# A sparse mixture's row scatters in four groups of four behind VectorE's work of four slots, and its gate's steps up to seven slots sooner

## The chip, the cores and the metric

One core of a Trainium2 chip runs the whole program in one launch. The metric is the time of one execution on the device in microseconds, taken as the median of several runs; lower is better. One further execution was recorded by the hardware profiler, and every row below is of that one.

## The reference, cut to what matters

Eight batches of attention between 512 positions and 32 states, in both directions, give 544 rows a batch, 4352 in all, of 512 numbers. A dense gated layer follows, and then a sparse one that sends every row to the one of eight experts with the largest logit.

```python
x = np.ascontiguousarray(attn_out.transpose(0, 2, 1, 3)).reshape(B * S, H * D)
a = x @ w_a
b = x @ w_b
x = (a * b @ w_out).astype(np.float32)
logits = x @ w_gate
e_idx = np.argmax(logits, axis=1)
gate_w = probs[np.arange(N), e_idx]
eom = 1.0 / (1.0 + np.exp(-(x @ w_output_gate)))
for e in range(E):
    mask = e_idx == e
    h = np.maximum(x[mask] @ w1[e], 0.0)
    ye = h @ w2[e]
    out[mask] = gate_w[mask, None] * eom[mask, e, None] * ye
```

Here probs is the softmax of the logits. All is float32; the kernel splits each factor of a large product into a high and a low part and adds three matmuls.

## The kernel before, in words

Phase 1 (class Phase1) does attention, the dense layer and the gate of the sparse layer; Phase 2 does the experts. Between them rows go through `ysort`, a table in memory that is sorted by expert: phase 1 scatters each row to its place there, phase 2 fetches the rows of one expert as blocks.

**A batch.** `main(b)` works through twelve blocks f of 128 hidden columns. `s1(b, f)` makes the two hidden products of the block on TensorE into `ps_ab` (12 matmuls each, L627); ScalarE copies one (`a`, L589), VectorE multiplies it by the other (L593), ScalarE rounds the result to the high part `gh` (L597), VectorE makes the low part `gl` (L601). `s2` (L646) adds the block's part of the output into the four banks `ps_y`. Each pair of blocks needs `Mh` and `Ml`, which `mprep` makes from the state and the weights: matmuls into two auxiliary banks `ps_m` (L566), ScalarE's copy `Mh` (L326), VectorE's difference `Ml` (L327).

**Slots.** Between these stand 24 slots, one behind each s1 and one behind each s2. `main` fills a list `prog` of 24 lists with small units of other work, and `slots` runs the units of the next slot each time that it is called. By the tables of `CFG`, `at` gives the slots of the next batch's attention (turning x, scores `ps_s`, softmax, the transposes `ps_e` at L486, the read of the states `ps_sr`), `gate` those of the gate of the batch before; the `ps_m` of the next pairs come every four slots, that of the next batch in slot 20. The scheduler keeps this order nearly as written on each engine, and moves an instruction only where its inputs are there sooner or later. All the small matmuls and transposes take turns in the two auxiliary banks of `ps_x`.

**The gate.** `gate(b, T)` returns nine units for T tiles of 128 rows: two that turn the output back into rows (`blocks`, in tile `y`, L810); `logits` (`ps_l`, L818); `gather` (transposes `ps_lt`, L831, and the sum L836); `pick` (the largest logit as a 0/1 row `oh`, L846 to L861); `osel` (the other gate's logit; GpSimd's running counts per expert, `cum` and `gpre`, L875 and L876); `scale` (the row's factor, L883 to L887, and the row's number, copied by GpSimd, L888); `pos` (place in the table: matmuls `ps_pos`, L895 and L898, and VectorE's L903 to L913); and `spread`. This last makes the places and factors stand where the rows stand (matmul `ps_sp`, L920), gets the places `gdu` as whole numbers (L924), writes the factors into the rows (L927), and has GpSimd issue 4T scatters of 128 pieces of 130 numbers each (L292):

```python
    def scatter(self, **kw):

        self.disjoint(self.nc.gpsimd.indirect_dma_start(**kw))
...
            nc.vector.tensor_copy(out=blocks[:, :, RB - 2 : RB - 1], in_=ps[:, n : 2 * n].unsqueeze(2))
            for t in range(n):
                self.scatter(
```

So a gate of four tiles issues sixteen scatters one behind the other, and L888 of the next gate, on the same queue, waits for all of them. The turns L810 of the next gate write the tile that they read, and wait for them too.

**Behind the batches.** `main_sr` runs the dense layer for the 256 rows that the states read, with the gate of the last batch in its own slots (`side`). Then comes a stage written out by hand in `moe_kernel`, with the gate of those 256 rows (two tiles, eight scatters in one unit, run inside `pre1(2)`), the table of the steps, and the first expert blocks; last `Phase2.run` loops over the other blocks.

`mark`, `follow`: `mark` gives the place in the program written so far, `follow(i, last)` keeps instruction i behind `last` on its engine without a wait.

Of the kernel before, what the change touches and what calls it, by code (L numbers as in the profile page):

```python
# [19 lines left out]
NB = 8  # L20
# [13 lines left out]
RB = DM // 4 + 2  # L34
# [10 lines left out]
    "conv": [0, 0, 0, 0, 0, 0, 0, 0, 0, 0, 1, 1, 1, 0, 1, 1, 1, 0, 0, 1, 0, 0, 0, 0],  # L45
    "at0": [12, 14, 13, 13, 15, 16, 16, 18, 18, 20, 21, 23, 23, 23],
    "at": [6, 7, 9, 10, 11, 13, 14, 17, 18, 15, 19, 21, 22, 23],
    "gate": [1, 2, 2, 5, 6, 7, 9, 10, 14],
    "u0": [10, 10, 11, 11],
    "sr0": 1,  # L50
    "mp0": 3,
# [4 lines left out]
class Phase1:  # L56
# [662 lines left out]
    def main_sr(self):  # L719
        nc, p1, p2 = self.nc, self.p1, self.p2  # L720
        n = self.nb * NS
        sh = p1.tile([P, 4, n], F32R, name="srh")
        sl_ = p1.tile([P, 4, n], F32R, name="srl")
        for j in range(4):
            self.split(sh[:, j, :], sl_[:, j, :], self.srT[:, j, :])
        g = self.gate(self.nb - 1, 4)
        choose, w1 = self.moe2.early()
        side = [[]] * CFG["sr0"] + [g[0:3], g[3:4], g[4:6], g[6:8], g[8:9], [choose]]
        side += [[]] * (18 - len(side)) + [[lambda j=j: w1(j)] for j in range(4)]
        aux = self.slots(side, 2 * NFC)  # L730
        gts = {}
        ys = [self.ps_y.tile([P, 512], F32, tag=f"y{t}", name=f"ps_y{t}")[:, 0:n] for t in range(4)]

        def wsplit(f):
            r = []
            for ab in range(2):
                h, l = (self.p3.tile([P, 4, P], F32R, tag=t, name=t) for t in ("wh", "wl"))
                self.split(h, l, self.wab[:, ab, :, P * f : P * f + P])
                r.append((h, l))
            return r  # L740

        w = wsplit(0)
        for f in range(NFC + 1):
            if f == NFC - 3:
                at = self.mark()
            if f < NFC:
                pab = []
                for ab in range(2):
                    ps = self.ps_ab.tile([P, 512], F32, tag="ab", name=f"ps_sab{ab}")
                    i = 0  # L750
                    wh, wl = w[ab]
                    for m, r in ((wh, sh), (wh, sl_), (wl, sh)):
                        for j in range(4):
                            nc.tensor.matmul(  # L754
                                out=ps[:, 0:n], lhsT=m[:, j, :], rhs=r[:, j, 0:n], start=i == 0, stop=i == 11
                            )
                            i += 1
                    pab.append(ps)
                if f + 1 < NFC:
                    w = wsplit(f + 1)  # L760
                gts[f] = self.product(pab[0], pab[1], n, f)
                next(aux)
            if f:
                self.s2(ys, gts.pop(f - 1), f - 1)
                next(aux, None)
        for _ in aux:
            pass
        for c, y in enumerate(ys):
            nc.scalar.activation(out=self.yTf[:, F2 + n * c : F2 + n * c + n], in_=y, func=AF.Copy)
        self.pin(at, nc.scalar, nc.vector)  # L770
# [29 lines left out]
    def gate(self, b, T):  # L800
        nc, p1, p2 = self.nc, self.p1, self.p2
        ident = self.ident
        st = {}

        yT = self.yT if T == 4 else self.yTf[:, 4 * T * P :].rearrange("p (c n) -> p c n", c=4)
        blocks = self.y[:, 0 : 4 * T]

        def turn(*cs):
            for c in cs:
                nc.vector.transpose(  # L810
                    out=blocks[:, :, 32 * c : 32 * c + 32], in_=yT[:, c, :].rearrange("p (t i) -> p t i", i=32)
                )
# [104 lines left out]
        def spread():  # L917
            n = 4 * T
            ps = self.aux("ps_sp")
            nc.tensor.matmul(  # L920
                out=ps[:, 0 : 2 * n], lhsT=self.turnto, rhs=st["z"].rearrange("p t g -> p (t g)"), start=True, stop=True
            )
            du = sm("gdu", [n], U32)
            nc.vector.tensor_scalar(  # L924
                out=du, in0=ps[:, 0:n], scalar1=4.0, scalar2=self.aoff[:, 0:1], op0=ALU.mult, op1=ALU.add
            )
            nc.vector.tensor_copy(out=blocks[:, :, RB - 2 : RB - 1], in_=ps[:, n : 2 * n].unsqueeze(2))  # L927
            for t in range(n):
                self.scatter(
                    out=self.ysort.rearrange("r (a w) -> (r a) w", a=4),  # L930
                    out_offset=bass.IndirectOffsetOnAxis(ap=du[:, t : t + 1], axis=0),
                    in_=blocks[:, t, :],
                    in_offset=None,
                    bounds_check=4 * NE * CAP - 1,
                    oob_is_err=False,
                )

        return [lambda: turn(0, 1), lambda: turn(2, 3), logits, gather, pick, osel, scale, pos, spread]


ds = bass.ds
# [11 lines left out]
class Phase2:  # L953
# [131 lines left out]
    def turn(self, e, y):  # L1085
        return e.transpose(out=self.yts, in_=y)
# [847 lines left out]
def moe_kernel(tc, x, state, w_a, w_b, w_out, w_gate, w_og, w1, w2, out):  # L1934
    w_a, w_b, w_out = (w.bitcast(I32) for w in (w_a, w_b, w_out))
    with ExitStack() as ctx:
# [5 lines left out]
        ph.run(ctx, m)  # L1942
        m.tiles(ctx)
        at = ph.mark()
        turn0, turn1, logits, gather, pick, osel, scale, pos, spread = ph.gate(NB, 2)
        table = m.table(cp)
        w2 = lambda c: m.wsplit(0, m.raw1[:, 1], c)
        turn = lambda i: m.turn(tc.nc.vector, m.yin[i])
# [15 lines left out]
        scale()  # L1964
        pos()
        stage()
        m.pre1(2, {6: spread})
        stage()
        m.fetch_pre(2)
        m.pre2(-2, 1)  # L1970
# [60 lines left out]
```

## Time and profile before

| what | us |
| --- | --- |
| median of 3 runs | 1182.87 |
| lowest and highest of them | 1180.47, 1192.52 |
| the profiled execution | 1190.98 |
| its span, from the first to the last instruction | 1189.3 |

TensorE's mean granted clock in the profiled execution was 0.978. A row of a timeline gives the start in us, the duration in us, the engine, the line, the operation with output and inputs, how many instructions were joined, and in brackets the idle time of the engine ahead of it with what ended that. Tiles go by their names in the program. A releaser "issue" means that the engine waited for nothing that the profile shows, "remote" that no event on this core was found for it. Matmuls overlap, so TensorE's durations add up to more than the time between starts.

### The profile page before, as it was taken

How to read it: one execution, taken by the hardware profiler on the slowest of the kernel's cores; microseconds unless marked ns; L12 is line 12 of the kernel's file. 1: busy time of each engine (PE TensorE's matmuls, PEld its weight loads, DVE VectorE, ACT ScalarE, POOL GpSimd, SP SyncE). 2: the span in 40 equal slices, each digit the busy share in tenths (PEclk: the TensorE clock that was granted, in tenths of full speed). 3: DMA queues.
4: the chain of work that ended last, by engine and by line, in shares of the span. 5: the costliest groups of instructions: out<-in, count | busy, mean ns of one | idle time of the engine just before them, and what ended most of it. 6: DMA issues, size and time to landing. Idle time of an engine off the chain costs nothing.

```text
span 1189.3 us, 19341 instructions
## 1 busy us (share of the span) xinstructions
PE 1127.1 (95%) x7032; PEld 900.1 (76%) x7032; DVE 627.6 (53%) x1108; ACT 431.8 (36%) x703; POOL 287.7 (24%) x393
## 2 busy tenths in 40 slices
PE   5999999999999989999999897989999999999996
PEld 3766776776777766767767686878899998989884
DVE  5987464465645634743654262773353354445455
ACT  6875333333333423333342232521231233233233
POOL 6000032050060240230410532122133212233111
PEclk7999999999999999999999997999999999999998
DMA  8653202103013022010000126237363143737421
GB/s 306 232 180 67 43 17 74 21 30 78 3 47 64 7 65 37 14 59 1 28 10 1 37 43 171 90 116 176 115 144 114 53 108 105 179 82 191 95 97 31
DMA packets 99519, 99.11 MB, mean 83 GB/s; under 512 B 60096, under 2 KB 71392, under 8 KB 99360
## 3 DMA queue, kind: packets, MB, share of 16 engines
q1 hardware_dynamic: 87976, 71.56, 22.3%
q0 software_dynamic: 11120, 25.52, 7.5%
q8 instruction: 82, 1.34, 0.5%
q14 instruction: 77, 0.63, 0.2%
q10 hardware_dynamic: 264, 0.07, 0.0%
HBM read 76.75 MB, written 21.02 MB: 82 GB/s over the span
## 4 chain that ended last, share of the span: by engine, by line
PE 84%; another core or an unknown queue 4%; DVE 4%; ACT 3%; issue 2%; DMA 2%; POOLq 0%; SPq 0%; DVEq 0%; POOL 0%; ACTq 0%
PE ps_ab L627 21%; PE ps_y L646 21%; PE ps_h L1149 15%; PE ps_o L1170 14%; PE ps_m L566 4%; PE ps_sab L754 2%; PE ps_h L1622 1%; PE ps_o L1622 1%; PE ps_l L818 1%; DMA yT<-in_moe_w_b 1%; PE ps_sr L501 1%; PE ps_e L486 1%; DMA y<-in_moe_w_a 1%; PE ps_s L368 1%
## 5 line engine op out<-in xcount | busy, mean ns | idle before, releaser
L1149 PE MATMUL ps_h<-yT,w 128*128 128x256 f32 x1536 | 196.7, 285 | 9.3 <-issue 5.1
L1149 PEld LDWEIGHTS ps_h<-yT,w 128*128 128x128 f32 x1536 | 192.7, 192 | 16.1 <-issue 6.0
L1170 PE MATMUL ps_o<-w,hT 128*128 (+1 forms) x768 | 188.5, 394 | 0.0
L292 POOL DMA_INDIRECT ysort<-y,gdu x136 | 149.1, 1097 | 149.0 <-DVE y L927 105.4
L646 PE MATMUL ps_y<-gh,wo_h 128*128 128x512 f32 (+1 forms) x432 | 167.8, 392 | 1.3 <-issue 0.7
L646 PE MATMUL ps_y<-gh,wo_l 128*128 128x512 f32 (+1 forms) x432 | 164.3, 384 | 0.6 <-issue 0.5
L646 PE MATMUL ps_y<-gl,wo_h 128*128 128x512 f32 (+1 forms) x432 | 163.0, 382 | 0.3 <-issue 0.3
L1170 PEld LDWEIGHTS ps_o<-w,hT 128*128 128x128 f32 x768 | 140.8, 189 | 28.2 <-DVE w L1044 0.4
L593 DVE TENSOR_TENSOR a<-a,ps_ab 128x512 f32<-128x512 f32 x96 | 65.6, 684 | 139.0 <-PE ps_ab L627 112.6
L627 PE MATMUL ps_ab<-Ah,Mh 128*128 128x512 f32 x384 | 128.9, 415 | 5.0 <-ACT a L589 3.0
L627 PE MATMUL ps_ab<-Al,Mh 128*128 128x512 f32 x384 | 121.2, 396 | 0.0
L627 PE MATMUL ps_ab<-Ah,Ml 128*128 128x512 f32 x384 | 119.9, 392 | 0.0
L1104 ACT ACTIVATE hT<-ps_h 128x512 fp32r<-128x512 f32 x64 | 38.1, 595 | 205.0 <-PE ps_h L1149 179.3
L1130 POOL DMA_INDIRECT out<-yT,gt x37 | 42.5, 1148 | 280.7 <-DVE yT L1120 230.0
L627 PEld LDWEIGHTS ps_ab<-Ah,Mh 128*128 128x128 f32 x384 | 66.4, 190 | 57.4 <-issue 41.1
L597 ACT ACTIVATE gh<-a 128x512 fp32r<-128x512 f32 (+1 forms) x108 | 65.5, 606 | 104.2 <-DVE a L593 103.5
L327 DVE TENSOR_TENSOR Ml<-ps_m,Mh 128x512 fp32r<-128x512 f32 x96 | 62.0, 685 | 77.2 <-ACT Mh L326 48.7
L646 PEld LDWEIGHTS ps_y<-gh,wo_h 128*128 128x128 f32 x432 | 81.9, 190 | 26.5 <-issue 5.4
L589 ACT ACTIVATE a<-ps_ab 128x512 f32<-128x512 f32 x96 | 57.3, 597 | 111.3 <-PE ps_ab L627 94.3
L1110 DVE SCALAR_TENSOR_TENSOR hT<-ps_h,hT 128x512 fp32r<-128x512 f32 x64 | 44.1, 688 | 100.2 <-ACT hT L1104 97.8
L646 PEld LDWEIGHTS ps_y<-gl,wo_h 128*128 128x128 f32 x432 | 81.8, 190 | 18.5 <-DVE gl L601 2.0
L601 DVE TENSOR_TENSOR gl<-a,gh 128x512 fp32r<-128x512 f32 (+1 forms) x108 | 71.1, 658 | 46.0 <-ACT gh L597 38.4
(271 smaller groups left out, 1399.8 us busy)
## 6 DMA issues: line engine op xcount, KB each, us to landing
raw<-in_moe_w SPq DMA_DIRECT2D x32, 512.0 KB
raw<-in_moe_w SPq DMA_DIRECT2D x8, 2048.0 KB
x<-in_x SPq DMA_DIRECT2D x7, 1024.0 KB
xin<-in_x SPq DMA_DIRECT2D x96, 64.0 KB
y<-ysort POOLq DMA_DIRECT2D x28, 128.0 KB, 3.5
y<-in_moe_w_a SPq DMA_DIRECT2D x6, 512.0 KB
yT<-in_moe_w_b SPq DMA_DIRECT2D x6, 512.0 KB
yT<-ysort POOLq DMA_DIRECT2D x24, 128.0 KB
```

What stands on the lines that cost most here:

```text
L292: self.disjoint(self.nc.gpsimd.indirect_dma_start(**kw))
L327: self.nc.vector.tensor_tensor(out=lo, in0=src, in1=hi.bitcast(F32), op=ALU.subtract)
L566: nc.tensor.matmul(out=ps[q][32 * j : 32 * j + 32, :].rearrange("n (a f) -> n a f", a=2), lhsT=st[64 * q : 64 * q + 64, 32 * j : 32 * j + 32],
L589: nc.scalar.activation(out=d["t"][:, 0:n], in_=d["p"][0][:, 0:n], func=AF.Copy)
L593: nc.vector.tensor_tensor(out=a, in0=a, in1=d["p"][1][:, 0:n], op=ALU.mult)
L597: nc.scalar.activation(out=d["g"][0][:, 0:n], in_=d["t"][:, 0:n], func=AF.Copy)
L601: nc.vector.tensor_tensor(out=gl[:, 0:n], in0=d["t"][:, 0:n], in1=gh.bitcast(F32)[:, 0:n], op=ALU.subtract)
L627: nc.tensor.matmul(out=ps, lhsT=m[:, ab, q, c0 : c0 + P], rhs=r[:, q, :], start=i == 0, stop=i == 5)
L646: nc.tensor.matmul(out=ys[c], lhsT=l[:, f, P * c : P * c + P], rhs=r, start=f == 0 and i == 0, stop=f == NFC - 1 and i == 2,)
L1110: return e.scalar_tensor_tensor(out=l, in0=self.ps_h[j % 2].rearrange("p (f n) -> p f n", f=2), scalar=0.0, in1=h.bitcast(F32), op0=ALU.ma ...
L1149: m = e.matmul(out=self.ps_h[j % 2][:, G * (f % 2) : G * (f % 2) + G], lhsT=self.w1[:, wh, x : x + P], rhs=self.yT[:, c, yh, :], start=k == 0,
L1170: m = e.matmul(out=self.ps_o[2 * (k % 2) + t], lhsT=self.hT[:, j % 2, f, hh, P * t : P * t + P], rhs=self.w2c(slot, wh, 2 * j + f), start= ...
```

## The change

The table `gate` has thirteen entries for thirteen units: the steps from `gather` on stand in slots 3, 4, 5, 6, 6 and 7 where they stood in 5, 6, 7, 9, 10 and 14. `spread` keeps the matmul and the places, and copies the factors aside (`gs`, in the tile of `gzv`, L928). The scatters are T further units `rows(k)` in slots 7, 11, 15 and 19: each copies the factors of its four pieces into the rows (L933), is kept behind the last VectorE instruction written before it, and issues four scatters. In `main_sr` all four groups stand in the slot where `spread` stood, in the two-tile gate both groups where `spread` was called.

```diff
--- before.py
+++ after.py
@@ -45,7 +45,7 @@
     "conv": [0, 0, 0, 0, 0, 0, 0, 0, 0, 0, 1, 1, 1, 0, 1, 1, 1, 0, 0, 1, 0, 0, 0, 0],
     "at0": [12, 14, 13, 13, 15, 16, 16, 18, 18, 20, 21, 23, 23, 23],
     "at": [6, 7, 9, 10, 11, 13, 14, 17, 18, 15, 19, 21, 22, 23],
-    "gate": [1, 2, 2, 5, 6, 7, 9, 10, 14],
+    "gate": [1, 2, 2, 3, 4, 5, 6, 6, 7, 7, 11, 15, 19],
     "u0": [10, 10, 11, 11],
     "sr0": 1,
     "mp0": 3,
@@ -725,7 +725,7 @@
             self.split(sh[:, j, :], sl_[:, j, :], self.srT[:, j, :])
         g = self.gate(self.nb - 1, 4)
         choose, w1 = self.moe2.early()
-        side = [[]] * CFG["sr0"] + [g[0:3], g[3:4], g[4:6], g[6:8], g[8:9], [choose]]
+        side = [[]] * CFG["sr0"] + [g[0:3], g[3:4], g[4:6], g[6:8], g[8:], [choose]]
         side += [[]] * (18 - len(side)) + [[lambda j=j: w1(j)] for j in range(4)]
         aux = self.slots(side, 2 * NFC)
         gts = {}
@@ -924,18 +924,29 @@
             nc.vector.tensor_scalar(
                 out=du, in0=ps[:, 0:n], scalar1=4.0, scalar2=self.aoff[:, 0:1], op0=ALU.mult, op1=ALU.add
             )
-            nc.vector.tensor_copy(out=blocks[:, :, RB - 2 : RB - 1], in_=ps[:, n : 2 * n].unsqueeze(2))
-            for t in range(n):
+            st["du"], st["gs"] = du, st["z"].rearrange("p t g -> p (t g)")[:, 0:n]
+            nc.vector.tensor_copy(out=st["gs"], in_=ps[:, n : 2 * n])
+
+        def rows(k):
+            n = 4 * k
+            at = self.mark()
+            i = nc.vector.tensor_copy(
+                out=blocks[:, n : n + 4, RB - 2 : RB - 1], in_=st["gs"][:, n : n + 4].unsqueeze(2)
+            )
+            ahead = [j for j in nc.cur_bb.bb.instructions[:at] if j.engine == nc.vector.engine]
+            self.follow(getattr(i, "ins", i), ahead[-1])
+            for t in range(n, n + 4):
                 self.scatter(
                     out=self.ysort.rearrange("r (a w) -> (r a) w", a=4),
-                    out_offset=bass.IndirectOffsetOnAxis(ap=du[:, t : t + 1], axis=0),
+                    out_offset=bass.IndirectOffsetOnAxis(ap=st["du"][:, t : t + 1], axis=0),
                     in_=blocks[:, t, :],
                     in_offset=None,
                     bounds_check=4 * NE * CAP - 1,
                     oob_is_err=False,
                 )
 
-        return [lambda: turn(0, 1), lambda: turn(2, 3), logits, gather, pick, osel, scale, pos, spread]
+        units = [lambda: turn(0, 1), lambda: turn(2, 3), logits, gather, pick, osel, scale, pos, spread]
+        return units + [lambda k=k: rows(k) for k in range(T)]
 
 
 ds = bass.ds
@@ -1942,7 +1953,7 @@
         ph.run(ctx, m)
         m.tiles(ctx)
         at = ph.mark()
-        turn0, turn1, logits, gather, pick, osel, scale, pos, spread = ph.gate(NB, 2)
+        turn0, turn1, logits, gather, pick, osel, scale, pos, *spread = ph.gate(NB, 2)
         table = m.table(cp)
         w2 = lambda c: m.wsplit(0, m.raw1[:, 1], c)
         turn = lambda i: m.turn(tc.nc.vector, m.yin[i])
@@ -1964,7 +1975,7 @@
         scale()
         pos()
         stage()
-        m.pre1(2, {6: spread})
+        m.pre1(2, {6: lambda: [u() for u in spread]})
         stage()
         m.fetch_pre(2)
         m.pre2(-2, 1)
```

VectorE, in the main of batch 2 (gate of batch 1; buffer numbers differ between the programs). Before, from the softmax's sums on; `gdu` holds the places, `y` the rows, `A` the softmax:

```order
L462 RECIPROCAL sm<-sm 128x32
L924 TENSOR_SCALAR gdu<-ps_sp,part 128x16
L927 COPY y<-ps_sp 128x16
L463 TENSOR_TENSOR A<-A,sm 128x1024
L509 RECIPROCAL s_2215<-s_2215 128x2
L449 STREAM_TRANSPOSE AT<-A 128x1024
L593 TENSOR_TENSOR a<-a,ps_ab_2351 128x512
L327 TENSOR_TENSOR Al<-AT,Ah 128x1024
L601 TENSOR_TENSOR gl<-a,gh 128x512
```

Now, from `a` of block 4 on:

```order
L593 TENSOR_TENSOR a<-a,ps_ab_2108 128x512
L924 TENSOR_SCALAR gdu<-ps_sp,part 128x16
L928 COPY gzv<-ps_sp 128x16
L933 COPY y<-gzv 128x4
L601 TENSOR_TENSOR gl<-a,gh 128x512
L327 TENSOR_TENSOR Ml<-ps_m_2155,Mh 128x2x256
L327 TENSOR_TENSOR Ml<-ps_m_2156,Mh 128x2x256
L593 TENSOR_TENSOR a<-a,ps_ab_2176 128x512
L601 TENSOR_TENSOR gl<-a,gh 128x512
L593 TENSOR_TENSOR a<-a,ps_ab_2211 128x512
L601 TENSOR_TENSOR gl<-a,gh 128x512
L933 COPY y<-gzv 128x4
```

And now at the batch's end:

```order
L593 TENSOR_TENSOR a<-a,ps_ab_2399 128x512
L601 TENSOR_TENSOR gl<-a,gh 128x512
L593 TENSOR_TENSOR a<-a,ps_ab_2438 128x512
L601 TENSOR_TENSOR gl<-a,gh 128x512
L933 COPY y<-gzv 128x4
L327 TENSOR_TENSOR Ml<-ps_m_2486,Mh 128x2x256
L327 TENSOR_TENSOR Ml<-ps_m_2487,Mh 128x2x256
```

The single copy L927 has become L928 and four L933; the first stands behind L924, the second ahead of the scores' copy, the last ahead of the next batch's `Ml`.

GpSimd, from the first scatter of a gate on, with the semaphores waited for (DMASW are the scatters' own, DVE VectorE's). Before:

```order
L292 DMA ysort<-y,gdu 147456x130 [waits DVE_49]
L292 DMA ysort<-y,gdu 147456x130 x7
L292 DMA ysort<-y,gdu 147456x130 [waits DMASW2_49]
L292 DMA ysort<-y,gdu 147456x130 [waits DMASW3_49]
L292 DMA ysort<-y,gdu 147456x130 [waits DMASW4_49]
L292 DMA ysort<-y,gdu 147456x130 [waits DMASW5_49]
L292 DMA ysort<-y,gdu 147456x130 [waits DMASW6_49]
L292 DMA ysort<-y,gdu 147456x130 [waits DMASW7_49]
L292 DMA ysort<-y,gdu 147456x130 [waits DMASW0_49]
L292 DMA ysort<-y,gdu 147456x130 [waits DMASW1_49]
L888 COPY y<-ids 128x16 [waits DMASW4_49,DMASW5_49,DMASW3_49,DMASW6_49,DMASW2_49,DMASW7_49,DMASW1_49,DMASW0_49]
```

Now:

```order
L292 DMA ysort<-y,gdu 147456x130 [waits DVE_49]
L292 DMA ysort<-y,gdu 147456x130 x3
L292 DMA ysort<-y,gdu 147456x130 [waits DVE_49]
L292 DMA ysort<-y,gdu 147456x130 x3
L292 DMA ysort<-y,gdu 147456x130 [waits DMASW2_49,DVE_49]
L292 DMA ysort<-y,gdu 147456x130 [waits DMASW3_49]
L292 DMA ysort<-y,gdu 147456x130 [waits DMASW4_49]
L292 DMA ysort<-y,gdu 147456x130 [waits DMASW5_49]
L292 DMA ysort<-y,gdu 147456x130 [waits DMASW6_49,DVE_49]
L292 DMA ysort<-y,gdu 147456x130 [waits DMASW7_49]
L292 DMA ysort<-y,gdu 147456x130 [waits DMASW0_49]
L292 DMA ysort<-y,gdu 147456x130 [waits DMASW1_49]
```

The same sixteen scatters; every fourth one now waits for VectorE.

TensorE, in the same main, from the counts' matmuls on. Before (`ps_s` are the next batch's scores):

```order
L895 MATMUL ps_pos<-goh,tri 128x32
L898 MATMUL ps_pos<-gpre,ones 128x32
L627 MATMUL ps_ab_2182<-Ah,Mh 128x512 x2
L627 MATMUL ps_ab_2182<-Al,Mh 128x512 x2
L627 MATMUL ps_ab_2182<-Ah,Ml 128x512 x2
L627 MATMUL ps_ab_2189<-Ah,Mh 128x512 x2
L627 MATMUL ps_ab_2189<-Al,Mh 128x512 x2
L627 MATMUL ps_ab_2189<-Ah,Ml 128x512 x2
L368 MATMUL ps_s_2203<-xT,stT 32x512
```

Now (`ps_st` is the transpose of the next batch's states):

```order
L895 MATMUL ps_pos<-goh,tri 128x32
L898 MATMUL ps_pos<-gpre,ones 128x32
L352 MATMUL ps_st<-ident,st_1859 128x128
L627 MATMUL ps_ab_2101<-Ah,Mh 128x512 x2
L627 MATMUL ps_ab_2101<-Al,Mh 128x512 x2
L627 MATMUL ps_ab_2101<-Ah,Ml 128x512 x2
L627 MATMUL ps_ab_2108<-Ah,Mh 128x512 x2
L627 MATMUL ps_ab_2108<-Al,Mh 128x512 x2
L627 MATMUL ps_ab_2108<-Ah,Ml 128x512 x2
L920 MATMUL ps_sp<-gzv,turnto 128x32
```

`ps_pos` now stands one s1 ahead of `ps_sp`, where two s1 lay between them.

## Rows read from the trace of the kernel before

**Rows 1.** The page's head and its busy time of each engine.

```profile
span 1189.3 us, 19341 instructions
...
PE 1127.1 (95%) x7032; PEld 900.1 (76%) x7032; DVE 627.6 (53%) x1108; ACT 431.8 (36%) x703; POOL 287.7 (24%) x393
```

**Rows 2.** Busy time by stretch: length, five engines, granted clock, DMA share, GB/s.

```profile
253.00:334.00 81.00, 80.04 (x495) 57.76 (x494) 44.03 (x83) 28.44 (x53) 20.06 (x26) 1.00 0.17 41
...
415.00:496.00 81.00, 75.89 (x460) 55.58 (x459) 39.80 (x77) 25.66 (x48) 15.25 (x23) 0.98 0.16 38
...
658.00:683.00 25.00, 20.00 (x97) 14.85 (x97) 6.22 (x9) 5.08 (x9) 13.84 (x15) 1.00 0.12 38
683.00:750.00 67.00, 57.32 (x419) 53.77 (x418) 31.46 (x81) 24.05 (x50) 19.09 (x26) 0.87 0.38 95
750.00:785.00 35.00, 30.52 (x206) 26.79 (x205) 23.99 (x63) 14.03 (x25) 9.08 (x14) 0.97 0.47 159
```

**Rows 3.** TensorE's waits, 172 to 683 us: total us, times, longest.

```profile
PE ps_e L486 <- DVE Ml L327: 5.1, 1, 5.1
PE ps_e L486 <- issue: 5.0, 5, 1.1
PE ps_ab L627 <- ACT a L589: 3.0, 1, 3.0
PE ps_ab L627 <- DVE a L593: 2.0, 1, 2.0
```

**Rows 4.** Timeline of TensorE at the end of one batch, and one batch later.

```profile
251.28 1.09 PE L566 MATMUL ps_m<-wab,stT 64*32 64x512 f32 x16
...
263.95 1.09 PE L566 MATMUL ps_m<-wab,stT 64*32 64x512 f32 x16
...
267.39 0.61 PE L627 MATMUL ps_ab<-Ah,Ml 128*128 128x512 f32 x2
268.96 0.66 PE L486 MATMUL ps_e<-ident,sc 128*128 128x128 f32 x4 [0.96 <-issue]
...
349.79 0.66 PE L486 MATMUL ps_e<-ident,sc 128*128 128x128 f32 x4 [0.98 <-issue]
```

**Rows 5.** Timeline of ScalarE: two copies in one batch, one later, the hand-written stage.

```profile
252.47 1.09 ACT L326 ACTIVATE Mh<-ps_m 128x512 fp32r<-128x512 f32 x2 [1.19 <-PE ps_m L566]
...
267.59 1.08 ACT L326 ACTIVATE Mh<-ps_m 128x512 fp32r<-128x512 f32 x2 [5.18 <-PE ps_ab L627]
...
433.37 1.08 ACT L326 ACTIVATE Mh<-ps_m 128x512 fp32r<-128x512 f32 x2 [9.11 <-remote]
...
781.62 0.60 ACT L1104 ACTIVATE hT<-ps_h 128x512 fp32r<-128x512 f32 x1 [8.97 <-remote]
```

**Rows 6.** Timeline of GpSimd: scatters of one batch, and of the last gate.

```profile
247.54 1.73 POOL L292 DMA_INDIRECT ysort<-y,gdu  x1 [15.12 <-DVE y L927]
...
264.28 0.97 POOL L292 DMA_INDIRECT ysort<-y,gdu  x1 [0.31 <-issue]
...
269.39 0.97 POOL L292 DMA_INDIRECT ysort<-y,gdu  x1 [0.30 <-DMA ysort<-y,gdu]
...
769.91 1.03 POOL L292 DMA_INDIRECT ysort<-y,gdu  x1 [2.28 <-DVE y L927]
```

**Rows 7.** Timeline of VectorE: the scatters' copy, then the gate's chain a batch later.

```profile
247.08 0.18 DVE L927 COPY y<-ps_sp 128x16 f32<-128x16 f32 x1
...
291.75 0.69 DVE L601 TENSOR_TENSOR gl<-a,gh 128x512 fp32r<-128x512 f32 x1 [0.70 <-ACT gh L597]
294.74 1.29 DVE L327 TENSOR_TENSOR Ml<-ps_m,Mh 128x512 fp32r<-128x512 f32 x2 [2.30 <-ACT Mh L326]
...
297.70 0.42 DVE L836 TENSOR_REDUCE gL<-ps_lt 128x64 f32<-128x256 f32 x1
...
300.66 0.18 DVE L887 RECIPROCAL gv<-gez 128x4 f32<-128x4 f32 x1
```

## The prediction

> **What bounds the kernel now.** I read the page's busy shares first, then the busy time by stretch, then TensorE's own waits, and last the timelines of TensorE, ScalarE and GpSimd over the end of one batch. TensorE is busy for 1127.1 of 1189.3 us [rows 1]: nothing shortens the run unless it takes idle time or work from TensorE. A batch takes 80.8 us (the same `ps_e` stands at 268.96 and 349.79 [rows 4]), of which an undisturbed one has 80.04 in 81 us busy; the stretch from 415 us has 75.89 us and a granted clock of 0.98, the last 25 us of the batches 20.00 us [rows 2]. After the batches come two more stretches with holes: 57.32 of 67 us at a clock of 0.87, and 30.52 of 35 us [rows 2]. TensorE's four longest waits between 172 and 683 us add up to 15.1 us [rows 3]: 5.0 us in five pieces "issue" and 5.1 us in one piece, all ahead of `ps_e`; and 3.0 and 2.0 us ahead of `ps_ab` in the last batch.
>
> The place of the regular one: `ps_m` of the next batch ends at 265.04 (263.95 + 1.09), the last `ps_ab` pair at 268.00, and the second `ps_e` starts only at 268.96 after 0.96 us of idle [rows 4]. It needs a PSUM bank that VectorE frees with `Ml`, which follows ScalarE's copy `Mh`. That copy starts at 267.59, 2.55 us after its matmul's end. The same pair earlier in the batch: `ps_m` ends at 252.37 (251.28 + 1.09), `Mh` starts at 252.47, 0.10 us later [rows 4, 5]. ScalarE is free for 5.18 us ahead of the late one, and its one wait there is for TensorE; so TensorE's announcement (the semaphore that its matmul raises) is late, not the work. In the batch from 415 us the same copy comes at 433.37 after 9.11 us of idle, and the releaser is one the profile can't name [rows 5].
>
> What stands beside it: GpSimd begins the batch's sixteen scatters at 247.54 and begins the last one at 269.39 [rows 6]. The on-time pair lies four scatters into this burst, the late one after the thirteenth scatter's start at 264.28 [rows 6]. So a burst of about four leaves TensorE's announcements on time, and one of thirteen makes them 2.5 us late. I read the 15.1 us as the price of the burst's length.
>
> **What the change removes.** Idle ahead of `ps_e`: 5.0 us (five batches), and 5.1 us in the batch from 415 us. Idle ahead of `ps_ab` in the last batch: 3.0 + 2.0 = 5.0 us. After the long stall the clock was 0.98 over 81 us, elsewhere in these batches 1.00 [rows 2], that is 0.02 x 81 = 1.6 us during which TensorE ran part of the time at the lower of its levels (1.2 instead of 2.4 GHz). Together 5.0 + 5.1 + 5.0 + 1.6 = 16.7 us, if a burst of four costs nothing. Bounds of that term: no gain if four scatters at the same place are late as well, and at most 16.7 us plus what the stretch from 683 us gives back. That stretch issues its sixteen scatters in one slot as before, and the eight of the last gate stay one burst; I take nothing there.
>
> **What it adds and moves.** Per gate of four tiles there are one copy of 16 columns (L928) and four of 4 columns (L933) where one copy (L927) stood; that one took 0.18 us [rows 7], so at most 5 x 0.18 - 0.18 = 0.72 us of VectorE per batch. VectorE is busy 44.03 of 81 us [rows 2], and no added copy feeds TensorE; without that cover it would be 7 x 0.72 = 5.0 us. Below nothing: L924 and the old copy leave the softmax's dense stretch, some 0.2 us each batch for instructions that TensorE doesn't wait for. I take 0.
>
> A scatter group waits for its own copy alone. GpSimd has nothing else queued behind the fourth group but the copy of row numbers, which waits for all landings already. With 24 slots in 80.8 us a slot is 3.4 us, so the groups start some 13 us apart. One scatter takes 0.97 us and 0.30 of issue [rows 6], a group thus 5.1 us, and 8 us lie between two groups. By the order the fourth copy stands behind slot 19, ahead of the `Ml` whose `ps_m` starts at 263.95 [rows 4]: its scatters run from about 264 to 269, where the last of the sixteen now starts at 269.39 [rows 6]. The next batch's turns of `y`, which need all landings, come no later than now.
>
> The gate's steps sooner: the logits' gather and VectorE's small chain from L836 (297.70) to L887 (ends 300.84) take 3.14 us with one `gl` among them, and move from behind slot 5 to behind slot 3. There VectorE has 294.74 - 291.75 = 2.99 us from the start of `gl` to that of the next `Ml`, and it sits idle for 0.70 us ahead of that `gl` [rows 7]: 3.7 us for 3.14. The two small exponentials now stand ahead of ScalarE's `Mh`; should the chain come out 0.5 us longer, `Ml` slips by that, and its first reader stands two slots behind it. `ps_pos` stands two slots behind the chain, `ps_sp` one slot behind `ps_pos`: between them lie chains of four to eight small instructions, 1 to 2 us if each is like the 0.18 us of L887 [rows 7], under 3.4 to 6.7 us of matmuls. I take 0; if each batch lost 0.5 us here, 3.5 us.
>
> **Sum.** The profiled execution took 1190.98 us: 1190.98 - 16.7 = 1174.3 us. It is 8.1 us above the median of 1182.87. I put this surplus to the stalls that came once (in the batch from 415 us 4.1 us over the regular 1.0, its 1.6 us of clock, and the last batch's 5.0, together 10.7 us): a median run then has 2.6 us of these, and loses 2.6 + 6.0 (six regular ones): again 1174.3 us. If a median run keeps its irregular stalls elsewhere, it is 1182.87 - 6.0 = 1176.9 us.
>
> **A rule that speaks against it.** The rows show ScalarE's copy 2.55 us behind its matmul late in the burst, 0.10 us early in it [rows 4, 5]. The Trainium skill (SBUF — State Buffer, "Who interferes with whom") says that TensorE and ScalarE never wait on any other user of SBUF, and that compute and DMA don't slow each other. By that rule the late copies are not the scatters' doing, and spreading these returns nothing: 1182.9 us, the third rival below. The trace doesn't bear it out for the announcements, whatever SBUF itself does.
>
> **Rivals.**
> First, the lateness belongs to the place, not to the length: the fourth group still runs beside the next batch's `Mh`. For it speaks that the lateness is seen there in every batch; also, in the last gate a burst of eight was enough, with ScalarE idle for 8.97 us up to 781.62, that is from 2.7 us after its first scatter at 769.91 [rows 5, 6] (other transfers ran there). Against it, the on-time pair at 252. The regular 6.0 us then stay and only the median's 2.6 us of long ones go: 1180.3 us.
> Second, more is gained: the profile's surplus lies in the stretch from 683 us (9.7 us of idle, clock 0.87 [rows 2]), so a median run has all 16.7 us in its batches: 1182.87 - 16.7 = 1166.2 us. If half the idle of that stretch goes too, since no late burst precedes it, 1161 us. For it: the clock of 0.87 is the biggest hole of the page. Against: its own burst is unchanged.
> Third, the lateness is not the scatters' doing but, say, the profiler's own, and no plain run has it: 1182.9 us. For it: the profiled execution is the slower one. Against: the plain ones lie 12 us apart, which even batches don't explain.
> Fourth, on the other side: announcements are late from a group's first scatters wherever the cover is thin, and there are now four such places in a batch, one of them ahead of the softmax's dense stretch. Price per group as the longest regular wait, 1.1 us [rows 3]: 4 x 7 x 1.1 = 30.8 us for 16.7, so 1182.87 + 14.1 = 1197 us. It decides as soon as four scatters make an announcement late by more than about 1.5 us; the pair at 252 speaks against it.
>
> **How the numbers follow.** Forecast 0.50 at 1174.3 (own range 1168 to 1179), place 0.14, more 0.20, not the scatters 0.08, slower 0.08. One per cent, about what a measurement of this kernel can tell from no change, is 1171.0 to 1194.7. Faster by more: the second rival and two fifths of the forecast, 0.20 + 0.20 = 0.40; slower: 0.08; the rest 0.52. The range takes in the second rival down to 1160 and the third, with a little for the unknown costs, up to 1184.
>
> **What would show it.** Right: in the changed kernel's batches no idle ahead of the second `ps_e`, `Mh` some 0.1 us behind its `ps_m`, 80 us per batch with even lengths, scatters in fours of about 5 us. The forecast is wrong if `Mh` at the batch's end is still 2 us late (first rival), if TensorE waits behind the first, second or third group (fourth), or if the waits are gone and the time is not (third). The gate's part is wrong if TensorE waits ahead of `ps_lt`, `ps_pos` or `ps_sp`.

## The result, and the profile after

The changed kernel took 1161.76 us (median of 6 runs, 1158.23 to 1166.81); the kernel before, run beside it, 1188.38 us (6 runs, 1180.47 to 1196.57). The ratio is 0.9756, 95% interval 0.9716 to 0.9795: faster, by more than forecast (1174.3 us). The profiled execution of the changed kernel took 1159.95 us.

The page's head and its busy time of each engine, now [rows 1]:

```profile
span 1158.4 us, 19399 instructions
...
PE 1115.9 (96%) x7032; PEld 894.4 (77%) x7032; DVE 632.3 (55%) x1142; ACT 431.9 (37%) x703; POOL 275.1 (24%) x393
```

Busy time by stretch, the same five stretches as [rows 2] at their new places (length, five engines, granted clock, DMA share, GB/s):

```profile
252.00:333.00 81.00, 81.00 (x507) 59.14 (x500) 46.45 (x91) 29.31 (x53) 18.25 (x26) 1.00 0.17 41
412.00:493.00 81.00, 81.00 (x501) 59.20 (x500) 45.41 (x88) 28.92 (x52) 19.05 (x27) 1.00 0.17 41
638.50:663.50 25.00, 25.00 (x122) 19.67 (x121) 7.66 (x13) 6.62 (x11) 7.78 (x8) 1.00 0.08 25
663.50:730.50 67.00, 59.19 (x436) 55.69 (x435) 32.68 (x87) 25.97 (x52) 19.98 (x28) 0.90 0.39 98
730.50:765.50 35.00, 30.13 (x201) 26.59 (x200) 24.65 (x72) 12.03 (x23) 8.73 (x12) 0.97 0.45 154
```

In the batches TensorE has no hole left: 81.00 of 81 us, at full clock. The list of its waits from 172 to 664 us, which held 15.1 us in four lines [rows 3], is empty. The two stretches behind the batches have nearly the holes of before.

The batch's end, where [rows 4, 5] show the late copy: TensorE, then ScalarE, then GpSimd's last group.

```profile
263.70 1.09 PE L566 MATMUL ps_m<-wab,stT 64*32 64x512 f32 x16
...
267.14 0.62 PE L627 MATMUL ps_ab<-Ah,Ml 128*128 128x512 f32 x2
267.59 0.60 PE L486 MATMUL ps_e<-ident,sc 128*128 128x128 f32 x4
```

```profile
264.88 1.09 ACT L326 ACTIVATE Mh<-ps_m 128x512 fp32r<-128x512 f32 x2 [2.71 <-PE ps_m L566]
```

```profile
263.25 0.97 POOL L292 DMA_INDIRECT ysort<-y,gdu  x1 [5.11 <-DVE y L933]
264.53 0.97 POOL L292 DMA_INDIRECT ysort<-y,gdu  x1 [0.30 <-issue]
```

`ps_m` ends at 264.79 (263.70 + 1.09), `Mh` starts at 264.88, 0.09 us later where it was 2.55 us, and the second `ps_e` starts without a wait. Two scatters of the last group had begun by then. The fours start at 224.04, 237.51, 253.12 and 263.25 in that batch.

Where the 30.9 us between the two spans (1189.3 and 1158.4) went, by the starts of the same instructions in both traces: from VectorE's first copy of batch 2's output (L660) to that of batch 8 ("batches"), from the first `ps_sab` to the first `ps_h` ("dense"), from there to the first `ps_tab` ("last gate"), and from there to the end ("experts"). The rest, the start and 0.6 us between the first two, changed by 0.3 us. Further rows are the runs that the next section tells of.

| kernel | batches | dense | last gate | experts |
| --- | --- | --- | --- | --- |
| before | 490.1 | 70.5 | 40.4 | 392.9 |
| changed | 471.0 | 68.4 | 41.0 | 382.9 |
| before_again | 486.7 | 70.3 | 40.4 | 392.8 |
| after_again | 471.1 | 68.1 | 41.6 | 387.2 |
| after_third | 471.1 | 67.8 | 40.9 | 386.1 |
| burst_slot14 | 493.2 | 67.9 | 41.5 | 381.1 |
| burst_slot7 | 535.4 | 68.4 | 41.8 | 390.5 |
| old_steps | 510.0 | 74.7 | 40.7 | 393.4 |
| eights | 471.3 | 68.4 | 41.7 | 387.1 |
| last_at_22 | 485.0 | 71.4 | 41.8 | 383.3 |
| twelve | 494.6 | 69.0 | 41.0 | 381.2 |
| groups_sr | 471.1 | 61.2 | 40.6 | 392.2 |
| sr_apart | 471.1 | 64.2 | 40.8 | 387.2 |
| sr_eights | 471.1 | 59.6 | 41.0 | 386.8 |

Between the first two rows: 19.1 us in the batches, 2.1 in the dense layer, -0.6 in the last gate, 10.0 in the experts, whose code the change doesn't touch.

### The profile page after: what moved, and what is told of

It is laid out like the page before. It is cut to its first block, busy times and chain, and to the rows that moved or that the text cites. A ratio compares the mean times of both kernels' runs of the same rounds, so it can differ in the third digit from the quotient of the medians.

```text
span 1158.4 us, 19399 instructions
## 1 busy us (share of the span) xinstructions
PE 1115.9 (96%) x7032; PEld 894.4 (77%) x7032; DVE 632.3 (55%) x1142; ACT 431.9 (37%) x703; POOL 275.1 (24%) x393
## 4 chain that ended last, share of the span: by engine, by line
PE 89%; DVE 3%; ACT 2%; DMA 2%; issue 2%; another core or an unknown queue 1%; SPq 0%; POOL 0%; DVEq 0%; POOLq 0%; ACTq 0%
PE ps_y L646 23%; PE ps_ab L627 22%; PE ps_h L1160 15%; PE ps_o L1181 14%; PE ps_m L566 4%; PE ps_sab L754 3%; PE ps_h L1633 2%; PE ps_o L1633 1%; DMA yT<-in_moe_w_b 1%; PE ps_t L1662 1%; DMA y<-in_moe_w_a 1%; PE ps_l L818 1%; PE ps_sr L501 1%; PE ps_s L368 1%
## 5 line engine op out<-in xcount | busy, mean ns | idle before, releaser
L1160 PEld LDWEIGHTS ps_h<-yT,w 128*128 128x128 f32 x1536 | 188.2, 190 | 13.4 <-ACT yT L1106 3.8
L1160 PE MATMUL ps_h<-yT,w 128*128 128x256 f32 x1536 | 191.7, 281 | 6.8 <-ACT yT L1106 3.4
L292 POOL DMA_INDIRECT ysort<-y,gdu x136 | 134.8, 991 | 239.0 <-DVE y L933 200.3
L646 PEld LDWEIGHTS ps_y<-gh,wo_l 128*128 128x128 f32 x432 | 82.0, 190 | 13.7 <-issue 0.4
```

Source lines behind the costliest of these rows:

```text
L646: nc.tensor.matmul(out=ys[c], lhsT=l[:, f, P * c : P * c + P], rhs=r, start=f == 0 and i == 0, stop=f == NFC - 1 and i == 2,)
L1160: m = e.matmul(out=self.ps_h[j % 2][:, G * (f % 2) : G * (f % 2) + G], lhsT=self.w1[:, wh, x : x + P], rhs=self.yT[:, c, yh, :], start=k == 0,
```

## The experiments

Four theories, named in the expectations. L: many scatters in a row make TensorE's announcements late, and the length of the row is what counts. G: the gain comes from the gate's steps standing sooner. P: the lateness belongs to the place at the batch's end. M: what counts is how many instructions TensorE gets through beside the scatters. On the experts' stretch, A: its length is an accident of one execution; B: the long rows of scatters make it long. Each edit is one to the changed kernel.

**One burst again, late.** The steps up to `pos` stay sooner; `spread` and all scatters stand in slot 14.

```diff
-    "gate": [1, 2, 2, 3, 4, 5, 6, 6, 7, 7, 11, 15, 19],
+    "gate": [1, 2, 2, 3, 4, 5, 6, 6, 14, 14, 14, 14, 14],
```

> The gate's steps sooner, but the places, the factors and all sixteen scatters stand in slot 14 again, as one burst. Theory L (the length of the burst makes TensorE's announcements late): batches of 80.3 to 80.8 us instead of 79.2, about 1 us of idle ahead of the second ps_e of each, Mh there some 2.5 us behind its ps_m, and once or twice a longer stall: 1176 to 1190 us where the changed kernel has 1161.8. Theory G (the gain comes from the gate's steps standing sooner): 1160 to 1166 us, batches of 79.2 us, no idle ahead of ps_e. For the stretch behind the table of steps (392.9 us before, 382.9 us now): theory A (an accident of a run) lets it come out anywhere from 382 to 394 us, theory B (the bursts' doing) near 393.

Measured: 1190.58 us (12 runs), just above the range of L, ratio to before 1.0054 (1.0022 to 1.0086). TensorE's waits from 195 to 689 us are those of [rows 3] again, and `Mh` at the end of batch 3 comes after 5.14 us of idle, 2.5 us behind its `ps_m`, which ends at 265.66:

```profile
PE ps_e L486 <- issue: 5.4, 4, 2.4
PE ps_e L486 <- DVE Ml L327: 5.2, 1, 5.2
PE ps_ab L627 <- ACT a L589: 4.5, 1, 4.5
```

```profile
268.18 1.08 ACT L326 ACTIVATE Mh<-ps_m 128x512 fp32r<-128x512 f32 x2 [5.14 <-PE ps_ab L627]
```

G falls: the sooner steps alone bring nothing. The row of sixteen alone brings the whole loss back, 22.2 us in the batches. For the experts B falls: 381.1 us with the long rows in every batch.

**One burst, early.** All four groups in slot 7.

```diff
-    "gate": [1, 2, 2, 3, 4, 5, 6, 6, 7, 7, 11, 15, 19],
+    "gate": [1, 2, 2, 3, 4, 5, 6, 6, 7, 7, 7, 7, 7],
```

> All four groups in slot 7, one burst of sixteen that is over some 20 us ahead of the batch's end. Theory L: Mh copies that fall behind the tenth scatter or so are late by 2 us and more, in the middle of the batch, where their readers stand two slots behind; the last Mh of the batch is on time, no idle ahead of ps_e; between 1161 and 1172 us, by whether a reader in the middle is reached. Theory P (lateness belongs to the place at the batch's end): no copy late anywhere, 1160 to 1164 us.

Measured: 1238.47 us, ratio 1.0456 (1.0414 to 1.0499). Both expected times are missed, and P's "no copy late anywhere" too; as L had it, the last `Mh` of the batch is on time, 0.1 us behind its `ps_m`, and no `ps_e` waits. The row of one batch runs from 233.65 to 253.83. TensorE there, then ScalarE, then VectorE:

```profile
243.96 0.61 PE L627 MATMUL ps_ab<-Ah,Ml 128*128 128x512 f32 x2
244.50 1.09 PE L368 MATMUL ps_s<-xT,stT 64*32 64x512 f32 x16
...
248.56 0.39 PE L646 MATMUL ps_y<-gl,wo_h 128*128 128x512 f32 x1 [0.57 <-issue]
249.29 0.47 PE L646 MATMUL ps_y<-gh,wo_h 128*128 128x512 f32 x1 [0.34 <-issue]
249.60 0.40 PE L646 MATMUL ps_y<-gh,wo_l 128*128 128x512 f32 x1
251.36 0.58 PE L646 MATMUL ps_y<-gl,wo_h 128*128 128x512 f32 x1 [1.37 <-issue]
257.07 2.58 PE L566 MATMUL ps_m<-wab,stT 64*32 64x512 f32 x16 [5.12 <-ACT sc L378]
```

```profile
249.34 0.60 ACT L589 ACTIVATE a<-ps_ab 128x512 f32<-128x512 f32 x1 [8.57 <-remote]
255.69 0.63 ACT L597 ACTIVATE gh<-a 128x512 fp32r<-128x512 f32 x1 [5.76 <-DVE a L593]
256.43 0.60 ACT L378 ACTIVATE sc<-ps_s 128x512 f32<-128x512 f32 x1
```

```profile
254.97 0.69 DVE L593 TENSOR_TENSOR a<-a,ps_ab 128x512 f32<-128x512 f32 x1 [13.48 <-remote]
```

`ps_ab` ends at 244.57 (243.96 + 0.61), and VectorE, idle since 241.49, reads it at 254.97, 10.4 us later. The scores end at 245.59 (244.50 + 1.09) and are copied at 256.43, 10.8 us later: that copy stands on ScalarE behind `gh`, which waits for VectorE's late `a`, so it can't be told how much of its delay is the scores' own. TensorE's own starts come apart, and the next `ps_m`, which needs the scores' bank, waits 5.12 us. So P falls: copies are late in the middle of the batch, and the one at its end is not. L's price was far too low: it had counted late copies, and not that TensorE itself stops, nor that banks in the middle of a batch are needed at once. The batches took 64.4 us more than the changed kernel's (535.4 - 471.0), at a granted clock of 0.94 over one of them:

```profile
204.00:294.00 90.00, 82.41 (x493) 58.39 (x493) 44.78 (x87) 28.46 (x51) 17.38 (x25) 0.94 0.15 36
```

**The old steps, the scatters in fours.**

```diff
-    "gate": [1, 2, 2, 3, 4, 5, 6, 6, 7, 7, 11, 15, 19],
+    "gate": [1, 2, 2, 5, 6, 7, 9, 10, 14, 14, 17, 20, 22],
```

> The gate's steps in their old slots 5, 6, 7, 9, 10 and 14, the four groups in 14, 17, 20 and 22. Theory L: 1160 to 1168 us, no idle ahead of ps_e, batches within 0.5 us of 79.2. Theory G: 1176 us or more. Rival P (the place at the batch's end): the last two groups run beside the last ps_m and Mh, so that Mh is late there by 2 us and TensorE idles 1 us in each batch: 1170 to 1176 us.

Measured: 1218.65 us, ratio 1.0287 (1.0245 to 1.0329), and not where any theory had it. `Mh` is on time and `ps_e` doesn't wait, against G and P; but slots 20 and 22 lie so close that the last eight scatters ran in one row, from 274.67 to 284.81, beside the 64 short matmuls of `ps_sr`, which took 6.39 us (278.41 to 284.80) where they take about 1.1:

```profile
278.41 0.86 PE L501 MATMUL ps_sr<-x,e2T 128*32 128x64 f32 x42
279.56 0.33 PE L501 MATMUL ps_sr<-x,e2T 128*32 128x64 f32 x6 [0.29 <-issue]
280.30 0.32 PE L501 MATMUL ps_sr<-x,e2T 128*32 128x64 f32 x5 [0.41 <-issue]
281.72 0.34 PE L501 MATMUL ps_sr<-x,e2T 128*32 128x64 f32 x5 [1.09 <-issue]
283.16 0.32 PE L501 MATMUL ps_sr<-x,e2T 128*32 128x64 f32 x4 [1.10 <-issue]
284.59 0.29 PE L501 MATMUL ps_sr<-x,e2T 128*32 128x64 f32 x2 [1.10 <-issue]
284.80 0.78 PE L646 MATMUL ps_y<-gh,wo_h 128*128 128x512 f32 x1
```

The batches take 510.0 us for 471.0, at a granted clock of 0.97 from 200 to 711 us. With the old steps and a slot or two between the groups, the last ones reach `ps_sr`; the sooner steps make the room that the groups need ahead of it. Whether the old steps would do with the groups in other slots wasn't tried.

**A second profile of both kernels.** Unchanged files.

> The kernel before once more, for a second profile of it. Theory A (the last stretch, from the table of steps on, takes 381 to 394 us by accident, whatever the scatters do; 392.9, 382.9, 381.1, 390.5, 393.4 and 392.2 us so far): it may come out anywhere in that band, and the batches take 488 to 494 us again, with about 1 us of idle ahead of the second ps_e and one or two long stalls. If the irregular stalls were this one execution's own: batches of 483 to 486 us, with regular idle times alone.

Measured: 1188.09 us in one run; batches 486.7 us, with stalls of 2.94 us ahead of a `ps_e` (in the batch from 415 us again) and 3.47 us ahead of a `ps_ab` in the last batch. That lies between the two expectations: the irregular stalls are no accident of the first profile, and they are somewhat smaller. The regular ones look otherwise than expected. Only one of the four regular batches has idle time ahead of `ps_e` (0.81 us); in the other three `Mh` is 1.0 us late, which reaches no reader, and `ps_sr`, just behind the row (its last scatter ends at 271.13 in this batch), stops twice, once for ScalarE's late `e2T`, and takes 2.1 us for 1.03:

```profile
271.90 0.42 PE L501 MATMUL ps_sr<-x,e2T 128*32 128x64 f32 x12
272.48 0.32 PE L501 MATMUL ps_sr<-x,e2T 128*32 128x64 f32 x4 [0.16 <-issue]
273.23 0.88 PE L501 MATMUL ps_sr<-x,e2T 128*32 128x64 f32 x48 [0.43 <-ACT e2T L493]
```

The four batches take 80.6 to 81.0 us all the same, 1.2 to 1.6 us more than in the changed kernel.

> The changed kernel once more. Theory A: batches within 1 us of 471.0 and the last stretch anywhere from 381 to 394 us; median 1158 to 1166 us, its spread of some 8 us being that of the last stretch.

Measured: 1161.39 us, ratio 0.9818 (0.9775 to 0.9861); batches 471.1 us, experts 387.2. As expected by A.

**Eight in a row, and twelve.** Two groups each in slots 7 and 15; then one group in slot 7 and three in slot 15.

```diff
-    "gate": [1, 2, 2, 3, 4, 5, 6, 6, 7, 7, 11, 15, 19],
+    "gate": [1, 2, 2, 3, 4, 5, 6, 6, 7, 7, 7, 15, 15],
```

> Two bursts of eight, in slots 7 and 15, for four groups of four. Theory L (only a long burst makes announcements late: four is safe, twelve is not): eight is still safe, batches within 0.5 us of 79.2, 1160 to 1167 us. Theory M (what counts is how many instructions TensorE gets through while a burst lasts; 48 matmuls beside eight scatters of the last gate were announced 5 us late): the bursts cover ps_m and some 45 matmuls each, announcements near their ends are late by 1 to 5 us, and the second reaches the batch's end: 1165 to 1185 us.

Measured: 1164.48 us, ratio 0.9843 (0.9799 to 0.9887); batches 471.3 us, no wait of TensorE in them. L was right for the batches: eight cost no more than four. They aren't without trace, though. TensorE and ScalarE at the end of one batch:

```profile
263.55 1.09 PE L566 MATMUL ps_m<-wab,stT 64*32 64x512 f32 x16
```

```profile
265.37 1.09 ACT L326 ACTIVATE Mh<-ps_m 128x512 fp32r<-128x512 f32 x2 [3.32 <-PE ps_m L566]
```

`ps_m` ends at 264.64 and `Mh` starts 0.7 us later, with the row over since 263.82; no start of TensorE is late for it.

```diff
-    "gate": [1, 2, 2, 3, 4, 5, 6, 6, 7, 7, 11, 15, 19],
+    "gate": [1, 2, 2, 3, 4, 5, 6, 6, 7, 7, 15, 15, 15],
```

> In the batches four scatters in slot 7 and twelve in a row in slot 15, over before ps_sr. Theory L with its edge between eight and twelve: the last Mh stands behind some nine scatters, late by 0.5 to 2.5 us, up to 1 us of idle ahead of ps_e: batches of 79.2 to 80.3 us, 1162 to 1172 us. If only the thirteenth and later ones do harm: 79.2 us, 1160 to 1165 us.

Measured: 1187.71 us, ratio 0.9950 (0.9916 to 0.9985); batches 494.6 us. GpSimd, TensorE and ScalarE at the end of one of them:

```profile
256.11 0.97 POOL L292 DMA_INDIRECT ysort<-y,gdu  x1 [24.12 <-DVE y L933]
...
267.16 0.97 POOL L292 DMA_INDIRECT ysort<-y,gdu  x1 [0.30 <-issue]
```

```profile
266.82 1.09 PE L566 MATMUL ps_m<-wab,stT 64*32 64x512 f32 x16
```

```profile
272.04 1.08 ACT L326 ACTIVATE Mh<-ps_m 128x512 fp32r<-128x512 f32 x2 [6.75 <-PE ps_ab L627]
```

The ninth of the row starts at 267.16, `ps_m` ends at 267.91 (266.82 + 1.09), and `Mh` starts at 272.04, 4.1 us late. So the edge lies between eight and twelve in a row, as the first of the two expectations had it; its size was again too small (up to 2.5 us of lateness and 1172 us expected). The count alone doesn't set the lateness: here nine scatters had begun when `ps_m` ended, in the kernel before twelve had, with 2.55 us in the first profile and 1.0 us in most batches of the second.

**The last group beside `ps_sr`.**

```diff
-    "gate": [1, 2, 2, 3, 4, 5, 6, 6, 7, 7, 11, 15, 19],
+    "gate": [1, 2, 2, 3, 4, 5, 6, 6, 7, 7, 11, 15, 22],
```

> The last group in slot 22 in place of 19, beside the 64 short matmuls of ps_sr (1.03 us now; 6 to 7 us with the last of eight scatters beside them). Theory L: a burst of four is safe wherever it stands, batches of 79.2 us, 1160 to 1166 us. Theory M: the short matmuls are held up until the group is over, 2 to 4.5 us in each of seven batches, with the clock falling behind it: 1176 to 1205 us.

Measured: 1183.37 us (12 runs), ratio 1.0021 (0.9986 to 1.0055); batches 485.0 us, 14 us more than the changed kernel's. The group of four starts at 273.11; TensorE:

```profile
273.57 1.12 PE L501 MATMUL ps_sr<-x,e2T 128*32 128x64 f32 x49
275.10 0.33 PE L501 MATMUL ps_sr<-x,e2T 128*32 128x64 f32 x5 [0.41 <-issue]
...
276.55 0.33 PE L501 MATMUL ps_sr<-x,e2T 128*32 128x64 f32 x5 [0.40 <-issue]
277.28 0.39 PE L646 MATMUL ps_y<-gh,wo_h 128*128 128x512 f32 x1 [0.40 <-issue]
```

M is right here: `ps_sr` takes 3.7 us (273.57 to 277.28) for 1.1, 2.6 us per batch. So the gain hung on slot 19: three slots later a group of four costs all of it (before, run beside it, took 1181.84 us), 14 us of it in the batches and 3.0 in the dense layer (71.4 us for 68.4).

**The dense layer.** The last gate's groups apart in `main_sr`'s side slots. The choice of the experts must stay behind the last scatter, since the weights that it loads overwrite rows not yet sent.

```diff
-        side = [[]] * CFG["sr0"] + [g[0:3], g[3:4], g[4:6], g[6:8], g[8:], [choose]]
+        side = [[]] * CFG["sr0"] + [g[0:3], g[3:4], g[4:6], g[6:8], g[8:10], [], g[10:11], [], g[11:12], [], g[12:] + [choose]]
```

> The changed kernel with the groups of the last batch's gate spread too, in side slots 5, 7, 9 and 11 of the dense layer of the 256 rows; the choice of the first experts stands behind them in slot 11 instead of 6. Theory L: the holes of TensorE in that stretch (58.59 us busy of 66.4) shrink by half or more, the stretch from the first ps_sab to the first ps_h takes 61 to 66 us instead of 68.4; the later choice costs nothing or up to 14 us behind it (the loads of weights start later by five slots): 1154 to 1172 us in all. If the holes there are not the scatters' doing: 68 to 69 us in the stretch, 1161 to 1176 us.

Measured: 1156.31 us, ratio 0.9766 (0.9725 to 0.9806); the stretch takes 61.2 us instead of 68.4, as L had it. The scatters ran as two rows of eight there, 2.2 us apart. Two variants, and the changed kernel beside them:

> The changed kernel a third time, beside the others of this call: 1158 to 1166 us, batches 471 us, the stretch from the first ps_sab to the first ps_h 68 us.

Measured: 1161.50 us (1159.41 to 1165.08), ratio 0.9722 (0.9687 to 0.9757).

```diff
-g[8:10], [], g[10:11], [], g[11:12], [], g[12:] + [choose]]
+g[8:10], [], [], g[10:11], [], [], g[11:12], [], [], g[12:] + [choose]]
```

> The changed kernel with the last gate's groups in side slots 5, 8, 11 and 14 of the dense layer of the 256 rows and the choice of the experts in 14, so that some 2.5 us and more lie between two groups. Theory L: that stretch takes 59 to 61 us (61.2 with slots 5, 7, 9 and 11), TensorE idles less than 1.5 us in it; with the loads of weights eight slots later nothing is lost as long as they land before their use: 1150 to 1157 us. If they land too late: up to 20 us behind the stretch.

Measured: 1160.44 us, ratio 0.9703 (0.9666 to 0.9741); 64.2 us in the stretch, outside the expectation. The scatters ran as two rows of eight after all, since VectorE's order puts the second and fourth copy further up; behind the second row's sixth scatter TensorE waited 4.48 us for ScalarE.

```diff
-g[8:10], [], g[10:11], [], g[11:12], [], g[12:] + [choose]]
+g[8:11], [], [], [], [], g[11:] + [choose]]
```

> The same with two bursts of eight, in side slots 5 and 10. Theory L (eight in a row are safe in the batches): the stretch takes 59 to 61 us, 1150 to 1157 us. Theory M (by TensorE's instructions: here a matmul starts every 0.12 us, twice as often as in the batches): the second half of each burst makes announcements late, 61 to 66 us in the stretch, 1154 to 1161 us.

Measured: 1155.24 us (1149.46 to 1156.58), ratio 0.9662 (0.9626 to 0.9697); 59.6 us in the stretch, as L had it. Its busy time, to be held against the fourth row of the changed kernel's table:

```profile
665.80:732.80 67.00, 62.46 (x503) 59.08 (x502) 42.31 (x102) 32.27 (x64) 20.14 (x27) 1.00 0.46 127
```

Its slowest run is faster than the changed kernel's fastest on the same chip: this version beats both kernels, by 6.3 us at the median. That three kernels with two rows of eight each take 59.6, 61.2 and 64.2 us suggests that eight is about the edge where a matmul starts every 0.12 us; that is a reading of three single profiles.

## Why the prediction was wrong

The mechanism was right and the size was not: 8.6 us forecast (1182.87 - 1174.3), 26.6 us between the medians.

- **What bounds the kernel: a long row of scatters beside TensorE.** Right. Bringing the row back brought the waits back (burst_slot14), eight are free in the batches and twelve are not. The first rival (the place) and the third (not the scatters' doing) fall with these runs. Not shown is that the announcement "is late, not the work": TensorE's own starts stop as well (burst_slot7, old_steps). The counts were off by one: `ps_m` at 251.28 ends with three scatters begun and not four, and the start at 264.28 is the twelfth, not the thirteenth. The rule of the Trainium skill that I weighed (SBUF — State Buffer, "Who interferes with whom") does not carry over: whatever holds at SBUF's ports, scatters hold up TensorE and its readers by up to 10.4 us here.
- **The sum of the batches.** 16.7 us forecast, 15.7 of it in the stretch of the table (one regular stall, at 187.56 us, stands ahead of it); 19.1 measured there. The batch with the long stall gave 6.8 us (442.4 - 356.4 = 86.0 before, 79.2 now) for 5.1 + 1.6, the last one 5.6 for 5.0. The four regular ones in that stretch gave 1.5 to 1.9 us (80.8 to 79.2 twice) instead of 1.0: in the batch from 275.6 us 1.14 us is the block of TensorE with the stall, the rest lies in pieces of 0.1 us and less between other blocks.
- **The step that failed: the median.** "I put this surplus to the stalls that came once ... a median run then has 2.6 us of these": so I took the 16.7 us from the profiled 1190.98 us, and at the median counted half of them as not there. The runs showed more of them. By the lengths of the batches the two irregular ones gave 10.7 us in the first profile (86.03 us for 80.98 in the regular ones, and 5.6 in the last batch), and 8.3 us in the second (1.5 and 6.8), for the 2.6 us. 1182.87 was a low draw of three: with three more runs of the same comparison the median is 1188.38, and among the six 1190.98 is ordinary. It is not so everywhere; in the three comparisons with the changed kernel (1161.76, 1161.39 and 1161.50 us) before took 1188.38, 1181.84 and 1196.08, a gain of 26.6, 20.5 and 34.6 us. Each is over twice the forecast's 8.6. How many stalls a run without the profiler has can't be seen. Taken from the median, the same 16.7 us give the second rival's 1166.2 us, 0.4% from the result.
- **The term left out: the experts.** 10.0 of the 30.9 us between the two profiles lie there, 392.9 to 382.9 us. Over all kernels it takes 381.1 to 393.4 us. Long rows in the batches don't set it: burst_slot14 and twelve have 381.1 and 381.2, groups_sr 392.2. About half of the 10.0 us is one stall some 315 to 320 us into the stretch, first in before, then in after_again:

  ```profile
  1116.88 1.97 PE L1149 MATMUL ps_h<-yT,w 128*128 128x256 f32 x10 [2.89 <-issue]
  ```

  ```profile
  1090.62 3.12 PE L1160 MATMUL ps_h<-yT,w 128*128 128x256 f32 x13 [3.35 <-issue]
  ```

  The pair of blocks around it takes 10.2 us in before, 4.6 more than its neighbours, and 10.7 in after_again, 5.2 more. The first profile of the changed kernel doesn't have this stall, its second and third have it: that part is not the change's doing. Some 4 us more are the slower of two rates (last section). Both profiles of before are at the long end, and the three of the changed kernel at 382.9 to 387.2; whether the change has a hand in the rest stays open.
- **What the change adds.** Right at nothing: no wait of TensorE ahead of `ps_lt`, `ps_pos` or `ps_sp`, fours of 5 us, 79.2 us a batch.
- **The stretch from 683 us.** "I take nothing there": 2.1 us came in the dense layer, -0.6 in the last gate. The second rival's 1161 us came nearest, and by luck: it needed half the idle time of that stretch to go, and of 9.7 us 7.8 stayed. Nor does the profile's surplus lie there, which was its first reason: the second profile of before has 70.3 us in the dense layer for 70.5. That idle time shrinks when the row there is split (4.5 us in sr_eights).
- **The slower rival.** It did not come about: TensorE has no wait beside any of the four groups. Four are not safe everywhere, though: last_at_22 shows four scatters costing 14 us in the batches where TensorE's matmuls are short.

## What to carry to other kernels

Where GpSimd issues many scatters in a row, look at how late the readers of TensorE's results start, in the middle of the row and at its end; here eight in a row were free beside matmuls that start every 0.23 us, twelve were not, and beside runs of short matmuls even four cost 2.6 us. Put the rows where TensorE's work is coarse and no reader is urgent. And before a gain read from one profiled execution is scaled down to a median, take a second profile: what looks like one execution's bad luck may be what every run has.

## What the runs showed of the hardware

- Beside scatters TensorE's recorded starts run ahead and then stop: 49 short matmuls in 1.12 us, then five every 0.73 us; in the row of eight, 42, and then about five every 1.43 us. In burst_slot7 the `ps_y` starts from 248.56 on lie 0.73, 0.31 and 1.76 us apart where 0.23 is usual. So 40 to 50 short matmuls seem to fit between a recorded start and what holds them up. Whether the announcements are late or the matmuls themselves run later than recorded, these runs don't tell apart; nor what GpSimd's scatters and TensorE share. It wasn't tried. Nor was it tried whether the edge above eight has to do with the scatters' semaphores: in a row of sixteen each from the ninth on waits for that of the one eight before it, as the order of GpSimd ahead of the prediction shows.
- After the held-up `ps_sr` of old_steps the next matmuls start 0.43 us apart (285.38, 285.81) for 0.23: from 284.80 to 288.00 us the granted clock is 0.51, the lower of its two levels, though TensorE is busy all the time there; the 0.94 over a batch of burst_slot7 has such a stretch in it (0.50 from 257 to 261 us, with TensorE busy for 3.93 of 4 us, behind the row).
- The experts' stretch has two rates with the granted clock at 1.00 and no waits. A pair of blocks, 24 `ps_h` and then 12 `ps_o`, takes 5.60 us in before (892.83 - 887.23) and 5.49 in the changed kernel (869.29 - 863.80). TensorE in before, then in the changed kernel:

```profile
887.23 2.99 PE L1149 MATMUL ps_h<-yT,w 128*128 128x256 f32 x24
...
892.83 2.99 PE L1149 MATMUL ps_h<-yT,w 128*128 128x256 f32 x24
```

```profile
863.80 2.91 PE L1160 MATMUL ps_h<-yT,w 128*128 128x256 f32 x24
...
869.29 2.91 PE L1160 MATMUL ps_h<-yT,w 128*128 128x256 f32 x24
```

  54 of 55 such blocks of `ps_h` had the slower rate in before's first profile and 17 of 55 in the changed kernel's, some 37 x 0.1 = 4 of the 10 us; in before_again 24 had it, in burst_slot14 none. What sets the rate stays open.
